# Cosine attention and a leaky-ReLU MLP on one core: row sums inverted on ScalarE, and a new order for batch 2's norms and batch 4's loads

## The chip, the cores and the metric

The kernel runs on one core of a Trainium2 chip. A core has TensorE (PE, matrix products into PSUM), VectorE (DVE), ScalarE (ACT, functions such as exp and ln), GpSimd (POOL) and SyncE (SP, here a queue that issues transfers). They run side by side, each works off its own instructions in order, and semaphores tie them together. Sixteen DMA engines move data. The metric is device time in microseconds of one execution of the whole kernel.

## The reference, cut to what matters

Inputs are q, k and v of shape (8 batches, 12 heads, 448 positions, 64), tau = 0.1, and two weight matrices.

```python
q_n = q / (norm(q, axis=-1) + 1e-06)
k_n = k / (norm(k, axis=-1) + 1e-06)
scores = matmul(q_n, k_n.transpose(0, 1, 3, 2)) / tau
attn = softmax(scores)                    # exp, row sum, division
x = matmul(attn, v)                       # heads put side by side: 3584 x 768
h = x @ w_in                              # 768 -> 2048
out = maximum(0.01 * h, h) @ w_out        # 2048 -> 768
```

The cosine of q and k lies between -1 and 1, so the kernel leaves the maximum out of the softmax: it takes the exponential of ten times the cosine, sums it, and multiplies the product with v by one over the sum.

## The kernel before

**Tiling.** A batch's 448 positions are 4 tiles of 112. Twelve heads make six pairs p and three groups g of two pairs. Per batch the attention runs over twelve *steps* n = 2p + half, and each step handles two of the four key tiles of one pair:

- `scores` (L206, in batch 0 `part_scores`, L224): TensorE multiplies the transposed, normalized k and q (`kT`, `qT`) into PSUM, in two tiles `sc`. The pool of these has two buffers.
- `exponential` (L234): ScalarE turns each tile into `pe`.
- After a group's second pair is through, two entries go into the list `owed`, and the next two steps each take one out with `weigh`. The first (s = 0) makes the group's row sums on TensorE (`sums`, L239 with `ones`), inverts them (`inverse`), makes the first half of the values (`values`, L239 with `v_bf`) and multiplies the two (`x_write`, L283, or L286 and L288 in even batches). The second (s = 1) makes the other half. Sums and values lie in PSUM tiles `pv`, of which there are two: the sums' tile becomes free for the second values when `inverse` has read it, and the first values' tile when `x_write` has. Groups 0 and 1 are weighed at steps 4, 5 and 8, 9 and group 2 at steps 0, 1 of the next batch.

`inverse` has two ways of doing it: in batch 0 ScalarE computes exp(-ln(sum)) (L264, L265), in the seven others VectorE takes the reciprocal (L267).

**The MLP as filling.** `layer1` (L311: six matmuls, then a leaky ReLU on ScalarE, L316) and `layer2` (L324: sixteen matmuls, a copy on ScalarE, L330, and stores from SP, L336) form one long list `dense`. After each step `fill(budget(b, n))` emits as much of it as a fixed budget says. In batches 1 to 7, where nothing is owed and layer 1 is next, a step holds its second exponential until a piece of the filling is out. Layer 1, layer 2 and batch 0 and 1's transposes on TensorE share a PSUM pool `mm` of two tiles. All this order is written at build time: nothing is scheduled while the kernel runs.

**The norms of the next batch.** While one batch is attended to, q and k of the next are made ready, in hand-placed calls after the steps: `early` for batches 0 and 1, `after_scores` for the later ones. The chain for q and for k is:

- `load`: a DMA issued by GpSimd (L92) that also rounds to bf16. `qk_bf` has four buffers, so batch 4's tiles take those of batch 2, once batch 2's multiplies have read them.
- `norm_sums`: squares (L124) and a reduce (L127) on VectorE.
- `norm_root`: ln and exp on ScalarE (L139, L140).
- `norm_inverse` (L144, L145) on VectorE, and `norm_apply` (L152), six multiplies with the inverse norm, on the engine that is handed over: V is VectorE, P is GpSimd.
- `turn`: a transposing DMA issued by SP (L169) into `qT` or `kT`. Scores of batches 2 to 7 wait for both. `turned` first clears a few columns with a memset on GpSimd (L163). Batches 0 and 1 are transposed on TensorE instead (`turn_pair`, L180).

In batch 1, batch 2's q is summed after step 3 and its k after step 5; q's root and its multiplies, on GpSimd, follow at step 6, k's root and its multiplies, on VectorE, at step 7, and both turns after step 9. Batch 4's loads stand at steps 0 and 1 of batch 2, and are the next DMAs on GpSimd's queue after the multiplies of batch 2.

Of the kernel before, what the change touches and what calls it, by code (L numbers as in the profile page):

```python
# [10 lines left out]
ACTF = mybir.ActivationFunctionType  # L11
# [5 lines left out]
def kernel(  # L17
# [18 lines left out]
    nc = tc.nc  # L36
    B, H, S, D = q.shape
# [46 lines left out]
    def load(b, what, g0=0, g1=G):  # L84
        src = {"q": q_r, "k": k_r, "v": v_r}[what]
        if (what, b) not in st:
            if what == "v":
                st[what, b] = vpool.tile([PK, H, NT, D], BF16, name="v_bf")
            else:
                st[what, b] = bfpool.tile([PK, H, NT, D], BF16, name="qk_bf")  # L90
        if g1 - g0 == G:
            nc.gpsimd.dma_start(out=st[what, b], in_=src[b])  # L92
            return
        for g in range(g0, g1):
            nc.gpsimd.dma_start(out=st[what, b][:, g::G], in_=src[b][:, g::G])
# [19 lines left out]
    def norm_squares(b, what, eng, g0=0, g1=G):  # L115
        if (what + "n", b) not in st:
            st[what + "n", b] = inp.tile([PK, G, 2, NT, 2, D], BF16, name=f"{what}_n")
            st[what + "i", b] = small.tile([PK, G, 4, NT], F32, name=f"{what}_ni")
        for g in range(g0, g1):
            x, sq = by_quad(st[what, b])[:, g], squares(b, what, g, g + 1)[:, 0]  # L120
            if eng is nc.scalar:
                nc.scalar.activation(sq, x, func=ACTF.Square)
            else:
                eng.tensor_mul(sq, x, x)  # L124

    def norm_reduce(b, what, g0=0, g1=G):
        nc.vector.tensor_reduce(  # L127
            st[what + "i", b][:, g0:g1].rearrange("p g a t -> p (g a) t"),
            squares(b, what, g0, g1).rearrange("p g a t d -> p (g a) t d"),
            axis=AX.X, op=ALU.add,  # L130
        )

    def norm_sums(b, what, g0=0, g1=G):
        norm_squares(b, what, nc.vector, g0, g1)
        norm_reduce(b, what, g0, g1)

    def norm_root(b, what, g0=0, g1=G):
        ni = st[what + "i", b][:, g0:g1]
        nc.scalar.activation(ni, ni, func=ACTF.Ln, bias=tiny[:PK])  # L139
        nc.scalar.activation(ni, ni, func=ACTF.Exp, scale=0.5)  # L140

    def norm_inverse(b, what, g0=0, g1=G):
        ni = st[what + "i", b][:, g0:g1]
        nc.vector.tensor_scalar_add(ni, ni, 1e-6)  # L144
        nc.vector.reciprocal(ni, ni)  # L145

    def norm_apply(b, what, eng, g0=0, g1=G):
        x, xn, ni = by_quad(st[what, b]), st[what + "n", b], st[what + "i", b]
        for g in range(g0, g1):
            for j in range(2):  # L150
                ni_j = ni[:, g, 2 * j : 2 * j + 2]
                eng.tensor_tensor(  # L152
                    out=xn[:, g, j].rearrange("p t h d -> p h t d"),
                    in0=x[:, g, 2 * j : 2 * j + 2],
                    in1=ni_j.unsqueeze(3).to_broadcast([PK, 2, NT, D]),
                    op=ALU.mult,
                )


    def turned(b, what):  # L160
        if (what + "T", b) not in st:
            xt = tpool.tile([128, NT * HP * PK + 16], BF16, name=f"{what}T")
            nc.gpsimd.memset(xt[:, NT * HP * PK :], 0.0)  # L163
            st[what + "T", b] = xt
        return st[what + "T", b]

    def turn(b, what):
        xn, xt = st[what + "n", b], turned(b, what)
        nc.sync.dma_start_transpose(  # L169
            out=xt[:, : NT * HP * PK].rearrange("p (c n) -> p c n", n=PK),  # L170
            in_=xn.rearrange("p g j t h d -> p (g j t h d)"),
        )
# [72 lines left out]
    def x_place(b):  # L245


        if b % 2 == 0:
            st["x", b] = xpool.tile([128, KT, 512], BF16, name="xT")
            st["x64", b] = cpool.tile([128, KT, 64], BF16, name="x64")  # L250
        else:
            st["x", b] = xpool.tile([128, KT, 512], BF16, name="xT")
            nc.gpsimd.tensor_copy(out=st["x", b][:, :, 0:64], in_=st["x64", b - 1])

    def sums(b, g, c0=0, c1=S):
        sm = ppv.tile([128, S], F32, name="pv")
        columns(sm, b, g, lambda a, ki: ones[:PK, :], c0, c1)
        return sm

    def inverse(b, g, sm, c0=0, c1=S):  # L260
        st["rs", b, g] = wk.tile([128, S], F32, name="rs")
        rs = st["rs", b, g][:, c0:c1]
        if b == 0:
            nc.scalar.activation(rs, sm[:, c0:c1], func=ACTF.Ln)  # L264
            nc.scalar.activation(rs, rs, func=ACTF.Exp, scale=-1.0)  # L265
        else:
            nc.vector.reciprocal(rs, sm[:, c0:c1])  # L267
        if ("x", b) not in st:
            x_place(b)

# [19 lines left out]
    def weigh(b, g, s, c0=0, c1=S):  # L290
        if s == 0:
            inverse(b, g, sums(b, g, c0, c1), c0, c1)
        x_write(b, g, s, values(b, g, s, None, c0, c1), c0, c1)
# [73 lines left out]
    V, P, A = nc.vector, nc.gpsimd, nc.scalar  # L367
# [45 lines left out]
    sm = sums(0, 0, *one)  # L413
# [11 lines left out]
    po = values(0, 0, 0, None, *one)  # L425
    part_scores(2, 1, *one)
    inverse(0, 0, sm, *one)
    part_scores(3, 0, *one)
    part_scores(3, 1, *one)
# [6 lines left out]
    sm = sums(0, 1, *one)  # L436
# [9 lines left out]
    sm = sums(0, 2, *one)  # L446
# [11 lines left out]
    def step(b, what, g0, g1, *steps):  # L458

        for name, eng in steps:  # L460
            if name == "squares":
                norm_squares(b, what, eng, g0, g1)
            elif name == "reduce":
                norm_reduce(b, what, g0, g1)
            elif name == "root":
                norm_root(b, what, g0, g1)
            else:
                norm_inverse(b, what, g0, g1)
                norm_apply(b, what, eng, g0, g1)

    def early(b, n):
        def both(to, g0, g1, name, eq=None, ek=None):
            step(to, "q", g0, g1, (name, eq))
            step(to, "k", g0, g1, (name, ek))

        if b == 0:
            if n == 0:
                both(1, 0, 1, "squares", P, P)
            elif n == 2:
                both(1, 0, 1, "reduce")  # L480
            elif n == 3:
                both(1, 1, 2, "squares", P, P)
            elif n == 4:
                both(1, 0, 1, "root")
            elif n == 5:
                both(1, 0, 1, "apply", V, P)
            elif n == 6:
                both(1, 1, 2, "reduce")
            elif n == 8:
                both(1, 1, 2, "root")  # L490
                both(1, 2, 3, "squares", P, P)
                load(2, "q")
            elif n == 9:
                both(1, 1, 2, "apply", V, P)
                load(2, "k")
            elif n == 11:
                both(1, 2, 3, "reduce")
        elif n == 0:
            both(1, 2, 3, "root")
            load(2, "v")  # L500
        elif n == 1:
            both(1, 2, 3, "apply", V, P)
            load(3, "q")
        elif n == 2:
            load(3, "k")
        elif n == 3:
            norm_sums(2, "q")
        elif n == 5:
            norm_sums(2, "k")
        elif n == 6:  # L510
            step(2, "q", 0, 3, ("root", A), ("apply", P))
        elif n == 7:
            step(2, "k", 0, 3, ("root", A), ("apply", V))
        elif n == 9:
            turn(2, "k")
            turn(2, "q")

    def after_scores(b, n):
        if b < 2:
            return early(b, n)  # L520
        if b + 2 < B and n < 2:
            load(b + 2, "qk"[n])
        if b + 1 == B:
            return
        if n == 2:
            load(b + 1, "v")
            norm_sums(b + 1, "q")
        elif n == 3:
            norm_sums(b + 1, "k")
        elif n == 4:  # L530
            norm_root(b + 1, "q")
        elif n == 5:
            norm_root(b + 1, "k")
            norm_inverse(b + 1, "q")
            norm_apply(b + 1, "q", P)
        elif n == 6:
            norm_inverse(b + 1, "k")
            norm_apply(b + 1, "k", P)
        elif n == 7:
            turn(b + 1, "q")  # L540
        elif n == 9:
            turn(b + 1, "k")
# [21 lines left out]
    for b in range(B):  # L564
        for p in range(HP):
            for half in range(2):
                n = 2 * p + half
# [56 lines left out]
```

## Time and profile before

| | before |
|---|---|
| time, median of 3 (lowest to highest) | 488.46 us (488.28 to 489.73) |
| span of the profiled execution | 487.8 us |
| VectorE, L267, 128x448 | x21, 62.1 us, 2955 ns each |
| ScalarE, L234, 112x896 | x168, 147.0 us, 918 ns each |
| VectorE, L152 (k), all shapes alike, 112x512 | x8, 9.8 us, 1278 ns each |
| GpSimd, L152 (q and k) | x36 and x40, 38.6 and 41.8 us |
| turns into kT and qT, issue to landing | x6 each, median 7.3 and 5.0 us |
| loads of whole q and k tiles, 672 KB, issue to landing | x6 each, median 8.0 and 11.4 us |

How to read the profile. An engine's busy time is that in which it executes, and the idle time before an instruction is put down to what released it last. In a list of waits the three numbers are the total in us, how often, and the longest. A timeline line has its start and its length in us, the engine, the line of the code, the operation, the output and the inputs, and how many instructions are merged into it. The chain of work that ended last is followed back from the end: at each moment it names the work that all later work waited for. PEclk is TensorE's granted clock as a share of the full one. Names of tiles are those of the program.

### The profile page before, as it was taken

To read this page: it belongs to the slowest core of one execution; us is meant where nothing else is said; L and a number is where in the kernel's file an instruction comes from. 1 tells how busy PE (TensorE), PEld (TensorE's weight loads), DVE (VectorE), ACT (ScalarE), POOL (GpSimd) and SP (SyncE) were. 2 spreads that over 40 slices of the span, in tenths; PEclk is the share of its full clock that TensorE was granted. 3 is DMA by queue.
4 is the path that set the end of the run, shared out by engine and by line. 5 is a ranking of instruction groups with operands and counts; after the bars stand their busy time and mean duration, and the time that the engine had idled before them with its cause. 6 is when DMAs were issued, how large, how long until landed. Compare 5 with 4: busy or idle time off the path is not lost.

```text
span 487.8 us, 8428 instructions
## 1 busy us (share of the span) xinstructions
PE 435.2 (89%) x3570; PEld 219.6 (45%) x3584; DVE 214.7 (44%) x255; ACT 273.0 (56%) x457; POOL 127.1 (26%) x146
## 2 busy tenths in 40 slices
PE   0789887564899999997899999999899999999996
PEld 0456553341344544453344544454344544554463
DVE  5935759942852059222952069216813203312000
ACT  3778466532466547843765557754775476543411
POOL 7655560620028010830047010900090000000000
PEclk9999899967899999998999999999999999999999
DMA  9999999097505925296506943343233210020022
GB/s 121 211 202 203 129 163 182 1 130 113 74 0 68 196 67 84 50 127 117 90 1 98 179 77 63 58 104 66 42 56 63 78 50 0 17 65 17 1 65 66
DMA packets 79364, 42.61 MB, mean 87 GB/s; under 512 B 35040, under 2 KB 78560, under 8 KB 79328
## 3 DMA queue, kind: packets, MB, share of 16 engines
q0 software_dynamic: 37728, 22.81, 34.3%
q1 hardware_dynamic: 41600, 19.28, 18.0%
q8 instruction: 28, 0.46, 0.4%
q14 instruction: 8, 0.07, 0.0%
HBM read 45.61 MB, written 11.01 MB: 116 GB/s over the span
## 4 chain that ended last, share of the span: by engine, by line
PE 75%; DMA 11%; DVE 7%; ACT 3%; SPq 2%; issue 1%; POOL 1%; POOLq 0%; ACTq 0%
PE mm L311 28%; PE mm L324 28%; PE pv L239 11%; PE sc L206 7%; DMA w_in_sb<-in_moe_w_in_dram 5%; DMA kT<-k_n 2%; DMA qT<-q_n 2%; DVE k_n L152 2%; ACT pe L234 2%; DMA qk_bf<-in_q_dram 1%; SPq L169 1%; DVE rs L267 1%; DVE q_n L152 1%; ACT hT L316 1%; DVE k_ni L127 1%
## 5 line engine op out<-in xcount | busy, mean ns | idle before, releaser
L234 ACT ACTIVATE pe<-sc 112x896 bf16<-112x896 f32 (+2 forms) x192 | 168.4, 917 | 22.0 <-PE sc L206 13.0
L311 PE MATMUL mm<-xT,w_in_sb 128*128 128x512 bf16 (+3 forms) x850 | 156.2, 334 | 4.2 <-ACT hT L316 1.7
L324 PE MATMUL mm<-w_out_sb,hT 128*128 128x384 bf16 x896 | 154.3, 328 | 0.0
L267 DVE RECIPROCAL rs<-pv 128x448 f32<-128x448 f32 x21 | 62.1, 2955 | 157.4 <-PE pv L239 157.4
L324 PEld LDWEIGHTS <-hT 128*128 128x128 bf16 x896 | 85.0, 98 | 67.8 <-issue 14.7
L311 PEld LDWEIGHTS <-w_in_sb 128*128 128x128 bf16 x864 | 77.6, 99 | 78.4 <-issue 19.8
L316 ACT ACTIVATE hT<-mm 128x512 bf16<-128x512 f32 (+3 forms) x144 | 71.6, 503 | 69.6 <-PE mm L311 69.3
L330 ACT COPY osb<-mm 128x384 f32<-128x384 f32 x56 | 26.8, 479 | 107.6 <-PE mm L324 77.3
L152 POOL TENSOR_TENSOR q_n<-qk_bf,q_ni 112x512 bf16<-112x512 bf16 x36 | 38.6, 1102 | 98.9 <-DVE q_ni L145 82.3
L206 PE MATMUL sc<-qT,kT 64*128 64x448 bf16 (+1 forms) x336 | 50.4, 365 | 14.8 <-ACT pe L234 6.1
L239 PE MATMUL pv<-pe,v_bf 112*32 112x448 bf16 (+2 forms) x864 | 50.0, 355 | 11.1 <-DVE rs L267 10.9
L152 POOL TENSOR_TENSOR k_n<-qk_bf,k_ni 112x512 bf16<-112x512 bf16 x40 | 41.8, 1073 | 6.8 <-DVE k_ni L145 6.8
L92 POOL DMA_DIRECT2D v_bf<-in_v_dram x8 | 7.6, 946 | 115.5 <-PE pv L239 115.3
L239 PEld LDWEIGHTS <-v_bf 112*32 112x32 bf16 x864 | 21.9, 102 | 32.5 <-issue 22.6
L206 PEld LDWEIGHTS <-kT 64*128 64x128 bf16 (+1 forms) x336 | 12.4, 99 | 45.9 <-issue 42.2
L286 DVE TENSOR_TENSOR xT<-pv,rs 128x384 bf16<-128x384 f32 (+2 forms) x30 | 14.1, 477 | 33.7 <-PE pv L239 21.6
L127 DVE TENSOR_REDUCE k_ni<-k_n 112x16 f32<-112x1024 bf16 (+1 forms) x12 | 27.4, 2282 | 0.9 <-POOL k_n L124 0.6
L127 DVE TENSOR_REDUCE q_ni<-q_n 112x16 f32<-112x1024 bf16 (+1 forms) x12 | 27.3, 2279 | 0.3
L239 PE MATMUL pv<-pe,ones 112*32 112x448 bf16 (+2 forms) x432 | 26.3, 364 | 1.1 <-ACT pe L234 1.1
L283 DVE TENSOR_TENSOR xT<-pv,rs 128x448 bf16<-128x448 f32 x24 | 15.0, 625 | 19.5 <-PE pv L239 18.2
L239 PEld LDWEIGHTS <-ones 112*32 112x32 bf16 x432 | 9.6, 101 | 14.8 <-issue 11.2
L180 PE MATMUL mm<-ident,q_n 112*128 112x112 bf16 x48 | 5.6, 254 | 10.8 <-DVE q_n L152 10.5
(50 smaller groups left out, 171.4 us busy)
## 6 DMA issues: line engine op xcount, KB each, us to landing
v_bf<-in_v_dram POOLq DMA_DIRECT2D x8, 672.0 KB, 7.7
qk_bf<-in_q_dram POOLq DMA_DIRECT2D x6, 672.0 KB, 8.0
qk_bf<-in_k_dram POOLq DMA_DIRECT2D x6, 672.0 KB, 11.4
w_in_sb<-in_moe_w_in_dram POOLq DMA_DIRECT2D x4, 768.0 KB, 20.3
w_out_sb<-in_moe_w_out_dram POOLq DMA_DIRECT2D x2, 1536.0 KB, 28.0
out_dram<-osb SPq DMA_DIRECT2D x16, 168.0 KB, 2.2
out_dram<-osb SPq DMA_DIRECT2D x16, 144.0 KB, 2.1
out_dram<-osb SPq DMA_DIRECT2D x16, 120.0 KB, 2.0
```

The costliest lines, as they stand in the source:

```text
L127: nc.vector.tensor_reduce(st[what + "i", b][:, g0:g1].rearrange("p g a t -> p (g a) t"), squares(b, what, g0, g1).rearrange("p g a t d -> ...
L152: eng.tensor_tensor(out=xn[:, g, j].rearrange("p t h d -> p h t d"), in0=x[:, g, 2 * j : 2 * j + 2], in1=ni_j.unsqueeze(3).to_broadcast([P ...
L206: nc.tensor.matmul(out=sc[:wide, a, :S], lhsT=kT[r, o : o + wide], rhs=qT[r, p * S : (p + 1) * S], start=True, stop=True,)
L234: nc.scalar.activation(out=pe, in_=sc, func=ACTF.Exp, scale=inv_tau)
L239: nc.tensor.matmul(out=dst[32 * a : 32 * a + 32, c0:c1], lhsT=weights(a, ki), rhs=st["pe", b, 2 * g + a // 2][:, ki, a % 2, c0:c1], start= ...
L267: nc.vector.reciprocal(rs, sm[:, c0:c1])
L283: nc.vector.tensor_mul(x[:, kt, 64:512], po, rs)
L286: nc.vector.tensor_mul(x[:, kt, c0:c], po[:, c0:c], rs[:, c0:c])
L311: nc.tensor.matmul(out=pm[:, :n], lhsT=w_in_sb[:, kt, m * 128 : (m + 1) * 128], rhs=st["x", b][:, kt, x0 : x0 + n], start=(kt == 0), stop= ...
L316: nc.scalar.activation(out=st["h", c][:, m, :n], in_=pm[:, :n], func=ACTF.Prelu, alpha=0.01)
L324: nc.tensor.matmul(out=po[:, :NH], lhsT=st["h", c][:, m, j0 : j0 + 128], rhs=w_out_sb[:, m, n * NH : (n + 1) * NH], start=(m == 0), stop=( ...
L330: nc.scalar.copy(out=osb, in_=po[:, :NH])
```

## The change

Three edits go together.

1. `inverse` uses ScalarE's ln and exp in every batch. This is to take the long reciprocals off VectorE, and with them the waits of TensorE for the sums' buffer.
2. Batch 2's norms are rearranged inside batch 1. k is summed a step earlier; q's and k's roots come at steps 5 and 6; both sets of multiplies are VectorE's, q's at step 6 and k's at step 7, so that VectorE and GpSimd don't multiply at the same time; q is turned at step 7 as soon as it is through, and k at step 8.
3. Batch 4's loads go from steps 0 and 1 of batch 2 to steps 3 and 4. On GpSimd's queue they then stand behind the load of batch 3's v, and are to run after batch 2's turns rather than beside them.

```diff
     def inverse(b, g, sm, c0=0, c1=S):
         st["rs", b, g] = wk.tile([128, S], F32, name="rs")
         rs = st["rs", b, g][:, c0:c1]
-        if b == 0:
-            nc.scalar.activation(rs, sm[:, c0:c1], func=ACTF.Ln)
-            nc.scalar.activation(rs, rs, func=ACTF.Exp, scale=-1.0)
-        else:
-            nc.vector.reciprocal(rs, sm[:, c0:c1])
+        nc.scalar.activation(rs, sm[:, c0:c1], func=ACTF.Ln)
+        nc.scalar.activation(rs, rs, func=ACTF.Exp, scale=-1.0)
...
         elif n == 3:
             norm_sums(2, "q")
+        elif n == 4:
+            norm_sums(2, "k")
         elif n == 5:
-            norm_sums(2, "k")
+            step(2, "q", 0, 3, ("root", A))
         elif n == 6:
-            step(2, "q", 0, 3, ("root", A), ("apply", P))
+            step(2, "k", 0, 3, ("root", A))
+            step(2, "q", 0, 3, ("apply", V))
         elif n == 7:
-            step(2, "k", 0, 3, ("root", A), ("apply", V))
-        elif n == 9:
+            step(2, "k", 0, 3, ("apply", V))
+            turn(2, "q")
+        elif n == 8:
             turn(2, "k")
-            turn(2, "q")
 
     def after_scores(b, n):
         if b < 2:
             return early(b, n)
-        if b + 2 < B and n < 2:
-            load(b + 2, "qk"[n])
+        n0 = 3 if b == 2 else 0
+        if b + 2 < B and n0 <= n < n0 + 2:
+            load(b + 2, "qk"[n - n0])
```

## The prediction

> **What bounds the kernel now.** I read the page first, for the shares and the clock.
>
> ```profile
> PE 435.2 (89%) x3570; PEld 219.6 (45%) x3584; DVE 214.7 (44%) x255; ACT 273.0 (56%) x457; POOL 127.1 (26%) x146
> ...
> PEclk9999899967899999998999999999999999999999
> ```
>
> TensorE is the bound, and no other engine is near it. The clock row is at 9 nearly everywhere, with one hollow in slices 8 to 10 (98 to 134 us). So I asked for the waits of TensorE, and then for the busy time by stage.
>
> ```profile
> PE pv L239 <- DVE rs L267: 10.9, 3, 8.8
> PE sc L206 <- ACT pe L234: 6.1, 8, 1.2
> PE sc L206 <- DMA qT<-q_n: 5.7, 1, 5.7
> PE sc L206 <- DMA kT<-k_n: 2.5, 1, 2.5
> ```
> ```profile
> 82.00:92.80 10.80, 8.68 (x118) 5.24 (x117) 10.20 (x13) 8.00 (x21) 3.01 (x3) 1.00 0.13 29
> 92.80:101.50 8.70, 0.00 (x0) 0.00 (x0) 8.69 (x6) 1.53 (x2) 7.28 (x8) 0.64 0.14 9
> 101.50:105.20 3.70, 3.66 (x36) 2.34 (x35) 1.25 (x2) 0.56 (x2) 0.00 (x0) 0.50 1.34 181
> 111.00:116.60 5.60, 0.00 (x0) 0.01 (x1) 0.00 (x0) 0.44 (x1) 0.00 (x0) 0.91 1.22 236
> 116.60:127.50 10.90, 10.17 (x72) 3.81 (x72) 7.09 (x7) 3.45 (x4) 0.94 (x1) 0.57 0.15 12
> 240.00:300.00 60.00, 59.73 (x463) 27.82 (x465) 30.16 (x30) 37.11 (x59) 15.46 (x18) 1.00 0.51 86
> ```
>
> Columns: stretch and length, busy us of TensorE, weight loads, VectorE, ScalarE, GpSimd, granted clock, DMA share, GB/s. From 240 us on TensorE is busy 59.7 of 60 us, so there is nothing to win there. The loss lies between 80 and 128 us, at the end of batch 1's attention: two stretches in which TensorE does nothing, each followed by one at a granted clock of 0.50 to 0.57. The VectorE timeline and the chain tell why.
>
> ```profile
> 85.36 3.35 DVE L127 TENSOR_REDUCE k_ni<-k_n 112x48 f32<-112x3072 bf16 x1
> ...
> 90.16 8.47 DVE L152 TENSOR_TENSOR k_n<-qk_bf,k_ni 112x512 bf16<-112x512 bf16 x6
> 98.55 2.94 DVE L267 RECIPROCAL rs<-pv 128x448 f32<-128x448 f32 x1
> ```
> ```profile
> 98.78 7.08 SPq L169
> ...
> 105.97 10.51 DMA qT<-q_n
> ```
>
> Batch 1's second reciprocal stands behind the six k multiplies of batch 2's norms. These take 8.47 us, because GpSimd does the six q multiplies at the same time (89.79 to 98.08). TensorE needs the sums' PSUM buffer, which the reciprocal releases, and stands for 8.8 us. Both turns are issued only at 98.78, together with batch 4's two loads (98.37 and 99.35), so qT lands at 116.48.
>
> **What the Trainium skill says.** "TensorE: Matmul & The Clock Gate", Part 1: after an idle window of about 3.4 us the array runs at half clock until it has been busy for such a window. The trace agrees in kind: 16 value matmuls take 1.68 us after the first stall against 0.93 us at 88.86. It disagrees on the duration: 10.9 us of low clock follow the second stall. "SBUF — State Buffer", SBUF: two separate sides: VectorE with two SBUF inputs and GpSimd lock a shared port pair against each other. The trace agrees: a multiply starts every 1.41 us beside GpSimd (8.47/6) but every 0.645 us alone (1.29 us for two at 66.93), and GpSimd's median is 1.486 us against 1.008 us (6.05/6 at 142.98). "DMA: Bandwidth & Descriptors", Issuing engines are not separate DMA queues: all share 16 DMA engines. The trace agrees: turns land in 15.3 and 10.5 us beside the loads, in 5.0 and 5.6 us without (batches 4 and 3, q). "ScalarE: Activation LUTs", What ACT_TABLE_LOAD costs: 186 ns + 0.833 ns per element, one load for ln and exp together. The trace has 381 and 417 ns at 256 columns for L264 and L265 and a single table load.
>
> **Part 1, the reciprocals.** 21 x 2955 ns = 62.1 us leave VectorE. ScalarE gets 21 pairs. From 192 to 256 columns L264 goes from 330 to 381 ns and L265 from 363 to 417 ns, so at 448 columns I take 381 + 192 x 0.80 = 534 ns and 417 + 192 x 0.84 = 579 ns; the skill's rule gives 559 ns for each. A pair costs some 1.1 us, 23 us in all, and ScalarE goes from 273 to 296 us, 63% of the shorter span. In later batches that is hidden: a step with sums runs about 6.0 us of TensorE work (0.48 scores + 1.63 sums and values + three layer-1 columns of 1.3), while ScalarE then has two exponentials (1.72), three activations (3 x 0.5) and the pair (1.1), 4.3 us. The pair stands behind the exponentials, and ahead of the activations that release layer-1's PSUM, which in the trace begin at about the time at which it would end (156.65 against 156.85 us at batch 2's step 8). I charge 0.5 us for all of batches 2 to 7; the bounds are 0 and 2.
>
> **Part 2, the new order of batch 2's norms.** I follow the queues from 73.7 us, where q's squares start as before (step n is the n-th half-pair of batch 1).
> - Step 4: the sums end at 76.4, and ScalarE, idle from 76.8, inverts them by 77.9. VectorE ends q's sums at 78.9, does x_write, and k's squares and reduce (1.89 + 3.35 - overlap) at 79.5 to 84.7. k's load needs to be there at 79.5: it was issued at 62.56 and landed 9.9 us later.
> - Step 5: the values needn't wait for L267, saving 1.45 us: TensorE is at step 6 by 81.3.
> - Step 6: k's root now waits on ScalarE for the reduce. Behind it are queued step 7's exponentials, and TensorE's next score buffer waits for these. With two exponentials, q's root and two activations ahead of it, ScalarE comes to k's root at 84.7, just as the reduce ends, but the first exponential of step 7 starts at 85.3 rather than at 84.35. The 1.45 us are nearly lost: step 8's second score pair begins at 87.4 against 87.77.
> - Step 8: the pair sits between exponentials and activations and is done at 90.5; layer 1 waits for its PSUM and step 9's scores start at 91.6 against 92.17.
> - VectorE: inverse of q (0.63) and six multiplies alone (6 x 0.645 = 3.9; at 688 ns each, 4.1) to 89.8; the same for k to 94.4. x_write of step 8 follows; its buffer is wanted only in batch 2, so nobody waits.
> - Step 9: the values go at 92.1, not at 101.54. Up to batch 2's first scores the trace has 110.92 - 101.54 = 9.4 us, of which 1.6 are low clock up to 105.2 (0.75 in the values, 0.84 in 18 matmuls: 2.10 against 0.84 for 12). So TensorE is there at 92.1 + 7.8 = 99.9, say 100.3 with the activations' queue.
>
> **Part 3, turns and loads.** qT is issued at 90 and kT at 94.6; nothing else is on the DMA (29 GB/s at 82 to 92.8). Alone a turn landed in 5.0 to 5.6 us: kT is in at 99.6 to 100.2. The two turns overlap by at most a fraction. I take 100.6 for batch 2's first scores against 116.62: **16.0 us**. Without a pause there is no low clock either. The stretch 116.62 to 127.53 then takes 0.48 + 1.63 + 0.48 + 0.87 + 2.71 = 6.2 us, by the later durations in the chain, not 10.9: **4.7 us** (it holds the third L267 wait, 0.71). Batch 4's loads now queue behind batch 3's v at step 3 of batch 2, ahead of the next multiplies on GpSimd by over 15 us. At 8.6 and 14.2 us to landing they are in before batch 3's turn, and norm sums want them a batch later: no cost. Batch 4's own kT wait (2.5 us at 222 to 225) stays, since it collides with batch 6's loads, which don't move.
>
> **Sum.** 16.0 + 4.7 - 0.5 = 20.2; 488.46 - 20.2 = 468.3.
>
> **The rivals.**
> - *The turn takes the stall's place.* kT lands 2 to 4 us later (median of all k turns 7.3), or step 7's wait cascades; TensorE pauses and the low clock returns for 3.7 us or more. For: a 2.5 us wait was enough at 225 us, where the clock is 0.59 for 4 us. Against: the loads are gone. 468.3 + 3 + 3 = 474.
> - *ScalarE becomes the limit in batches 2 to 7.* Most of 18 pairs of 1.1 us comes onto the path: 468.3 + 15 = 483. Against: 37 us of 60 busy.
> - *Slower than before.* All 23 us come onto the path, and the late kT stalls with low clock (6): 468.3 + 23 + 6 = 497. It needs both to fail; nothing in the profile speaks for it but the 6.1 us of waits for L234.
> - *All stalls vanish.* 1.45 + 8.79 + 5.70 + 1.6 + 4.7 = 22.2 and nothing is charged: 466.
>
> **How the numbers follow.** Forecast 0.62, late turn 0.20, everything vanishes 0.11, ScalarE limit 0.04, slower 0.03. The range goes from 465.5 (the last rival with the measurement's width) to 475 (the late turn). Faster 0.96, same 0.01, slower 0.03.
>
> **What would show it.** The wait of L239 for VectorE is gone; the VectorE multiplies of batch 2 take about 0.65 us each and GpSimd's are away; both turns of batch 2 land within 6 us and the first wide scores start at 100 to 101 us with a clock of 1.0; L264 and L265 at 448 columns last 530 to 580 ns; ScalarE's wait for k's reduce is under 1 us. I am wrong if the first wide scores wait for kT by over 2 us, if the low clock is still there after 100 us, or if the waits for L234 and L316 grow by over 2 us after 130 us.

## The result and the profile after

The changed kernel takes 467.75 us (median of 4, 466.62 to 468.35) against 488.37 us before: 20.6 us less, a ratio of 0.958 with a 95% interval of 0.954 to 0.962. The prediction said 468.3 us and a gain of 20.2 us.

Times from here on are those of each kernel's own profile, and line numbers shift in the changed code: L308 and L321 are layers 1 and 2 (before: L311 and L324), L313 and L327 their work on ScalarE, L263 and L264 the ln and exp, L280 and L283 the products with the row sums' inverse. The profile after runs 1.22 us ahead of the one before when step 3 of batch 1 starts (71.78 against 73.00 us), from the loads at the start of the kernel (TensorE's first wait for the weights `w_in` is 0.25 us instead of 1.33). The code up to there is the same in both kernels, so this isn't the work of the change, and stages are compared by their length.

First TensorE's waits in the changed kernel (total us, times, longest):

```profile
PE mm L180 <- DVE q_n L152: 10.8, 2, 10.5
PE sc L206 <- ACT pe L234: 6.5, 9, 1.2
PE sc L206 <- DMA kT<-k_n: 2.3, 1, 2.3
```

The two big waits of before, 10.9 us for the reciprocal and 5.7 us for qT, are not in the list at all. The 10.5 us at the kernel's start and batch 4's wait for kT (2.3 us here, 2.5 us in the kernel before) were there before.

Then four stages, before and after: step 3 to step 9 of batch 1, step 9 to batch 2's first scores, these to batch 2's step 2, and all the rest (columns as in the prediction):

```profile
73.00:92.17 19.17, 14.41 (x176) 8.13 (x174) 18.39 (x20) 12.84 (x25) 2.55 (x3) 1.00 0.73 118
92.17:116.62 24.45, 9.75 (x89) 6.04 (x87) 10.57 (x8) 7.43 (x16) 7.91 (x9) 0.77 0.88 121
116.62:127.53 10.91, 10.20 (x73) 3.80 (x74) 7.12 (x7) 3.45 (x4) 0.94 (x1) 0.58 0.15 12
127.53:487.80 360.27, 348.38 (x2603) 167.27 (x2616) 133.62 (x129) 202.27 (x323) 71.73 (x83) 1.00 0.38 69
```
```profile
71.78:89.94 18.16, 14.62 (x176) 8.16 (x174) 17.92 (x25) 14.76 (x29) 0.25 (x3) 1.00 0.77 125
89.94:98.33 8.39, 8.03 (x88) 4.90 (x86) 3.79 (x7) 6.78 (x15) 0.00 (x0) 1.00 0.95 163
98.33:104.61 6.28, 6.25 (x73) 3.02 (x74) 2.96 (x5) 4.73 (x7) 2.33 (x3) 1.00 0.20 36
104.61:464.90 360.29, 348.67 (x2603) 167.35 (x2616) 81.86 (x111) 220.03 (x359) 72.21 (x84) 0.99 0.41 73
```

The gain is 1.0 us in the first stage, 16.1 in the second and 4.6 in the third, and nothing in the 360 us after it. The rest loses 52 us of VectorE (133.6 to 81.9) and gains 18 us of ScalarE (202.3 to 220.0), and its length doesn't move by 0.1 us. These 21.7 us and the 1.22 us at the start make up the 22.9 us between the two profiled spans. The medians lie only 20.6 us apart: the profiled runs took 489.77 and 466.62 us, the long end of the one kernel's runs and the short end of the other's.

VectorE in the changed kernel, where the reciprocal stood behind 8.47 us of multiplies:

```profile
80.14 3.35 DVE L127 TENSOR_REDUCE k_ni<-k_n 112x48 f32<-112x3072 bf16 x1
...
84.64 3.70 DVE L152 TENSOR_TENSOR q_n<-qk_bf,q_ni 112x512 bf16<-112x512 bf16 x6
...
88.96 3.70 DVE L152 TENSOR_TENSOR k_n<-qk_bf,k_ni 112x512 bf16<-112x512 bf16 x6
92.58 1.15 DVE L280 TENSOR_TENSOR xT<-pv,rs 128x448 bf16<-128x448 f32 x2
```

Twelve multiplies on one engine (8.0 us with the inverse between them) take no longer than six on each of two engines did (8.47 us), and q is through after the first half. The two products at 92.58 come late, and no one waits for them. SP's queue and TensorE's arrival at batch 2 show that both then come out at the same moment:

```profile
88.49 3.26 SPq L169 DMA_TRANSPOSE qT<-q_n  x1
92.73 3.92 SPq L169 DMA_TRANSPOSE kT<-k_n  x1
```
```profile
95.63 2.77 PE L321 MATMUL mm<-w_out_sb,hT 128*128 128x384 bf16 x16
98.33 0.55 PE L206 MATMUL sc<-qT,kT 64*128 64x448 bf16 x4
98.82 0.94 PE L239 MATMUL pv<-pe,ones 112*32 112x448 bf16 x16
```

The turns land 5.1 and 5.3 us after issue, kT thus at 98.0 us; TensorE is there at 98.3.

### The profile page after: what moved, and what is told of

Same layout as the page of the kernel before. It is cut to its first block, busy times and chain, and to the rows that moved or that the text cites. A ratio compares the mean times of both kernels' runs of the same rounds, so it can differ in the third digit from the quotient of the medians.

```text
span 464.9 us, 8442 instructions
## 1 busy us (share of the span) xinstructions
PE 429.8 (92%) x3570; PEld 217.6 (47%) x3584; DVE 151.4 (33%) x240; ACT 293.3 (63%) x499; POOL 118.7 (26%) x140
## 4 chain that ended last, share of the span: by engine, by line
PE 81%; DVE 7%; ACT 5%; DMA 3%; issue 1%; POOL 1%; SPq 0%; POOLq 0%; ACTq 0%; DVEq 0%
PE mm L308 30%; PE mm L321 30%; PE pv L239 12%; PE sc L206 8%; ACT pe L234 4%; DMA kT<-k_n 2%; DVE q_n L152 2%; DVE k_ni L127 1%; PE sc L224 1%; DVE q_ni L127 1%; PE mm L180 1%; ACT hT L313 1%; DMA qk_bf<-in_q_dram 1%; DVE q_ni L144 1%; DVE q_n L124 1%
## 5 line engine op out<-in xcount | busy, mean ns | idle before, releaser
L234 ACT ACTIVATE pe<-sc 112x896 bf16<-112x896 f32 (+2 forms) x192 | 168.4, 918 | 11.2 <-PE sc L224 7.6
L308 PE MATMUL mm<-xT,w_in_sb 128*128 128x512 bf16 (+3 forms) x850 | 155.6, 332 | 3.0 <-ACT hT L313 1.5
L321 PE MATMUL mm<-w_out_sb,hT 128*128 128x384 bf16 x896 | 154.4, 328 | 0.0
L321 PEld LDWEIGHTS <-hT 128*128 128x128 bf16 x896 | 85.0, 98 | 67.9 <-issue 14.7
L308 PEld LDWEIGHTS <-w_in_sb 128*128 128x128 bf16 x864 | 76.8, 98 | 77.0 <-issue 18.9
L313 ACT ACTIVATE hT<-mm 128x512 bf16<-128x512 f32 (+3 forms) x144 | 71.4, 502 | 48.1 <-PE mm L308 47.3
L327 ACT COPY osb<-mm 128x384 f32<-128x384 f32 x56 | 26.8, 479 | 96.6 <-PE mm L321 92.3
L206 PE MATMUL sc<-qT,kT 64*128 64x448 bf16 (+1 forms) x336 | 49.4, 357 | 9.3 <-ACT pe L234 6.5
L283 DVE TENSOR_TENSOR xT<-pv,rs 128x384 bf16<-128x384 f32 (+2 forms) x30 | 14.1, 477 | 126.8 <-ACT rs L264 93.7
L280 DVE TENSOR_TENSOR xT<-pv,rs 128x448 bf16<-128x448 f32 x24 | 14.8, 623 | 124.2 <-PE mm L308 47.3
L152 POOL TENSOR_TENSOR q_n<-qk_bf,q_ni 112x512 bf16<-112x512 bf16 x30 | 30.3, 1040 | 79.6 <-DVE q_ni L145 79.6
L239 PE MATMUL pv<-pe,v_bf 112*32 112x448 bf16 (+2 forms) x864 | 47.8, 344 | 0.2 <-ACT rs L263 0.2
L239 PE MATMUL pv<-pe,ones 112*32 112x448 bf16 (+2 forms) x432 | 24.5, 343 | 0.8 <-ACT pe L234 0.8
L180 PE MATMUL mm<-ident,q_n 112*128 112x112 bf16 x48 | 5.6, 254 | 11.0 <-DVE q_n L152 10.8
L264 ACT ACTIVATE rs<-rs 128x448 f32<-128x448 f32 (+2 forms) x27 | 14.4, 535 | 0.9
```

The source lines that it names most:

```text
L152: eng.tensor_tensor(out=xn[:, g, j].rearrange("p t h d -> p h t d"), in0=x[:, g, 2 * j : 2 * j + 2], in1=ni_j.unsqueeze(3).to_broadcast([P ...
L206: nc.tensor.matmul(out=sc[:wide, a, :S], lhsT=kT[r, o : o + wide], rhs=qT[r, p * S : (p + 1) * S], start=True, stop=True,)
L234: nc.scalar.activation(out=pe, in_=sc, func=ACTF.Exp, scale=inv_tau)
L239: nc.tensor.matmul(out=dst[32 * a : 32 * a + 32, c0:c1], lhsT=weights(a, ki), rhs=st["pe", b, 2 * g + a // 2][:, ki, a % 2, c0:c1], start= ...
L280: nc.vector.tensor_mul(x[:, kt, 64:512], po, rs)
L283: nc.vector.tensor_mul(x[:, kt, c0:c], po[:, c0:c], rs[:, c0:c])
```

## The experiments

The theory: two stalls follow one another, the sums' buffer behind VectorE's queue and the turns beside the loads, and each leaves TensorE at a low clock. Removing the first lets the second grow. The main rivals: the reciprocals alone were the cost; or the loads alone; or ScalarE's added work takes part of the gain back.

### The three edits apart

**Edit 1 alone**, on the kernel before:

```diff
-        if b == 0:
-            nc.scalar.activation(rs, sm[:, c0:c1], func=ACTF.Ln)
-            nc.scalar.activation(rs, rs, func=ACTF.Exp, scale=-1.0)
-        else:
-            nc.vector.reciprocal(rs, sm[:, c0:c1])
+        nc.scalar.activation(rs, sm[:, c0:c1], func=ACTF.Ln)
+        nc.scalar.activation(rs, rs, func=ACTF.Exp, scale=-1.0)
```

> The kernel before with edit 1 alone: row sums on ScalarE, batch 2's norms and batch 4's loads as before. Theory (two stalls in a row, the second set by the turns): the 8.8 us wait for the sums' buffer goes, but both turns still start when VectorE is through with k's multiplies, at about 97 us, and run beside batch 4's loads, so they land at 113 to 115 us and TensorE waits some 14 us there instead of 8.8 + 5.7, with the low clock after it. 486 to 488 us, a gain of 0 to 2 us. Rival (the reciprocals were the cost, 62 us of VectorE with TensorE waiting behind them): 468 to 475 us.

Measured: 484.12 us, ratio 0.993 (0.990 to 0.996). The first stall is gone and the second has eaten it; TensorE's waits in this kernel:

```profile
PE sc L206 <- DMA qT<-q_n: 13.9, 1, 13.9
PE mm L180 <- DVE q_n L152: 10.6, 1, 10.6
```

13.9 us instead of 8.8 + 5.7, as expected. kT landed 14.2 us and qT 9.4 us after issue. The time is 2 us below what was expected, and the profile has it in the stretch after the wait: 7.8 us from batch 2's first scores to its step 2 (113.25 to 121.07), not 10.9. The rival that all 62 us of reciprocals counted is out.

**Edit 3 alone**, on the kernel before:

```diff
-        if b + 2 < B and n < 2:
-            load(b + 2, "qk"[n])
+        n0 = 3 if b == 2 else 0
+        if b + 2 < B and n0 <= n < n0 + 2:
+            load(b + 2, "qk"[n - n0])
```

> The kernel before with edit 3 alone. Theory: the 8.8 us wait for the sums' buffer stays, but the turns issued at 98.8 us land alone, by 108 us, before TensorE is there at 110.9; the 5.7 us wait and the low clock after it go: 478 to 480 us. Rival (the turns are late because they are issued late): 486 to 488 us.

Measured: 481.99 us, ratio 0.989 (0.986 to 0.993), 2 us short of the expectation. The turns land in 5.3 and 6.8 us and TensorE doesn't wait for them. The rival is out. But the stretch after batch 2's first scores takes 9.75 us:

```profile
110.32 0.55 PE L206 MATMUL sc<-qT,kT 64*128 64x448 bf16 x4
...
114.80 0.94 PE L239 MATMUL pv<-pe,v_bf 112*32 112x448 bf16 x16 [1.82 <-DVE rs L267]
115.68 4.46 PE L324 MATMUL mm<-w_out_sb,hT 128*128 128x384 bf16 x16
```

With TensorE at full clock here (1.00 from 110.32 to 115.68), the third reciprocal is less hidden: the wait for it is 1.82 us, not 0.71. A low clock follows this wait (0.61 from 115.68 to 120.07): the 16 layer-2 matmuls take 4.46 us instead of the 2.77 of full clock.

**Edits 2 and 3**, the changed kernel with the VectorE reciprocal back (the reverse of the first diff):

> The changed kernel with edit 1 taken back: VectorE's reciprocal in batches 1 to 7, edits 2 and 3 kept. Theory: batch 1's second reciprocal stands behind both sets of multiplies and ends at about 100 us, TensorE waits 6 to 7 us for the sums' buffer, then runs 9.4 us to batch 2's first scores at about 109 us, where the turns are long there. 477 us, about half of the gain. Rival A (the new order alone does it): 468. Rival B (the reciprocal alone does it): 488.

Measured: 480.44 us, ratio 0.984 (0.978 to 0.990), 3 us over the expectation. TensorE's waits in this kernel:

```profile
PE pv L239 <- DVE rs L267: 6.9, 3, 3.6
PE sc L206 <- ACT pe L234: 6.0, 8, 1.2
PE mm L311 <- ACT hT L316: 3.4, 2, 3.0
```

The second reciprocal ended at 100.0 and batch 2's first scores went at 109.19, both as worked out. The wait divides otherwise: 3.0 us of it is earlier, because ScalarE stands at k's root until VectorE is through with k's reduce, which the first reciprocal has delayed by 3 us. What was missed comes afterwards, the same 1.82 us and slow layer-2 block as with edit 3 alone (9.75 us again, against 6.28 in the changed kernel). So edit 2 leans on edit 1: with reciprocals on VectorE, the earlier root blocks ScalarE.

**Edits 1 and 2**, the changed kernel with batch 4's loads back at steps 0 and 1:

```diff
-        n0 = 3 if b == 2 else 0
+        n0 = 0
```

> The changed kernel with edit 3 taken back: batch 4's loads at steps 0 and 1 of batch 2. Theory: GpSimd issues them as soon as batch 2's multiplies have read the tiles, at about 88 and 93 us, beside the turns, which land in 10 to 15 us instead of 5.1 and 5.3. Batch 2's first scores go at 104 to 107 us instead of 98.3, followed by the low clock (4 us more): 476 to 480 us. Rival (the turns were late only because they were issued late, the loads beside them cost little): 468 to 470 us.

Measured: 477.29 us, ratio 0.978 (0.972 to 0.984), as expected. GpSimd issues the loads at 88.90 and 93.21 us, each some 0.2 us after a turn; qT lands in 9.4 and kT in 14.0 us. TensorE's waits, and the stretches around the wait for kT:

```profile
PE sc L206 <- DMA kT<-k_n: 9.8, 2, 7.3
```
```profile
99.80:107.06 7.26, 0.00 (x1) 0.01 (x2) 0.00 (x0) 0.48 (x1) 0.00 (x0) 0.85 1.21 194
107.06:111.00 3.94, 3.94 (x36) 1.24 (x36) 0.00 (x0) 2.84 (x4) 0.00 (x0) 0.50 0.00 0
```

**Edits 1 and 3**, the old order of batch 2's norms:

> The changed kernel with edit 2 taken back: edits 1 and 3 with the old order of batch 2's norms. Theory: k's multiplies still run beside GpSimd's, the turns are issued at 96.5 and 100 us and the second lands at 105 us, where TensorE has been waiting since 99.4 us, with some low clock after it: 475 to 477 us. Rival (the new order adds nothing once the loads are away): 467 to 470 us.

Its edits are the first two diffs together. Measured: 474.06 us, ratio 0.973 (0.970 to 0.977), 1 us below the expectation. The turns land in 5.3 and 5.1 us, but are issued only at 96.51 and 99.95 us, and TensorE waits for the second:

```profile
PE sc L206 <- DMA qT<-q_n: 5.8, 1, 5.8
```

In us saved of 488, by the ratios: edit 1 alone 3.6, edit 3 alone 5.2, 1 and 3 13.0, 1 and 2 10.8, 2 and 3 7.8, all three 20.5. What an edit is worth depends on which of the others is there: edit 1 brings 3.6 us alone and 12.7 us as the last of the three.

### GpSimd's share of the multiplies

```diff
             step(2, "k", 0, 3, ("root", A))
-            step(2, "q", 0, 3, ("apply", V))
+            step(2, "q", 0, 3, ("apply", P))
```

> The changed kernel with q's multiplies of batch 2 on GpSimd again, at the new place, so that they run beside VectorE's for k. Theory[...]: six k multiplies take 8.5 us and six q multiplies 8.7 us, both from about 84.7 us, so both turns are issued at 93.5 to 97 us and kT lands at about 102 us, 3.6 us after TensorE is there; with some low clock 471 to 475 us. Rival (no contention; GpSimd is only slower, 1.0 us each): q is through at 91 us, k at 89 us, kT lands by 99.5 us, 468 to 469 us.

Measured: 472.54 us, ratio 0.969 (0.963 to 0.976), as the theory had it. GpSimd's and VectorE's multiplies in this kernel:

```profile
84.77 7.85 POOL L152 TENSOR_TENSOR q_n<-qk_bf,q_ni 112x512 bf16<-112x512 bf16 x6 [13.27 <-PE sc L206]
```
```profile
86.38 7.39 DVE L152 TENSOR_TENSOR k_n<-qk_bf,k_ni 112x512 bf16<-112x512 bf16 x6
```

1.23 us each on VectorE and 1.31 on GpSimd, against 0.62 and 1.01 alone. kT lands at 101.3 us, 3.3 us later than in the changed kernel, and TensorE waits 2.2 us:

```profile
101.37 0.55 PE L206 MATMUL sc<-qT,kT 64*128 64x448 bf16 x4 [2.16 <-DMA kT<-k_n]
101.85 0.94 PE L239 MATMUL pv<-pe,ones 112*32 112x448 bf16 x16
```

Dividing the work over two engines that hinder each other costs some 5 us by the medians. The profiled run, with 470.2 us the shortest of the five, shows some 3 us of it, in the start of batch 2's first scores (101.37 against 98.33 us). The low clock that was expected after the wait isn't in this profile (1.00 from 101.37 to 112 us), so where the other 2 us of the median go is open.

### Is the low clock an echo of the idle time?

The kernel before, with matmuls that do nothing for the result in the two idle stretches:

```diff
+    def busy(n):
+        pm = pmm.tile([128, 512], F32, name="mm")
+        for _ in range(n):
+            nc.tensor.matmul(
+                out=pm, lhsT=w_in_sb[:, 0, 0:128],
+                rhs=w_in_sb[:, 1, 0:512], start=True, stop=True,
+            )
...
+                if (b, n) == (2, 0):
+                    busy(30)
                 hold = b > 0 and not owed and dense[at[0]][1] < 2.0
...
+                if (b, n) == (1, 9):
+                    busy(38)
                 if owed:
                     weigh(*owed.pop(0))
```

> The kernel before with 68 matmuls more, whose results nothing reads: 38 of 512 columns ahead of step 9's values in batch 1 and 30 ahead of batch 2's first scores, where TensorE stands still. Theory (the low clock is the echo of the idle stretches): TensorE stays at the full clock, step 9's stretch gets 1.6 us shorter, which the wait for the turns takes up again, and the stretch after batch 2's first scores takes 7 us instead of 10.9: 483 to 485 us, faster with more work. Rival (the clock has other causes, or the matmuls are in the way): 488 to 490 us.

Measured: 485.12 us, ratio 0.995 (0.993 to 0.997): faster with 68 matmuls more, and 0.1 us above the range that was expected. Stretches of this kernel over the two stalls and the time after the second:

```profile
92.50:101.50 9.00, 9.00 (x48) 3.93 (x44) 9.00 (x6) 2.26 (x4) 8.11 (x9) 1.00 0.07 4
101.50:111.00 9.50, 8.78 (x89) 5.51 (x89) 1.78 (x3) 5.37 (x12) 0.00 (x0) 1.00 1.37 157
111.00:117.00 6.00, 5.38 (x25) 2.23 (x23) 0.00 (x0) 0.00 (x0) 0.00 (x0) 1.00 1.29 232
117.00:128.00 11.00, 8.49 (x84) 3.73 (x85) 8.76 (x7) 5.37 (x8) 0.93 (x1) 1.00 0.36 47
```

The granted clock is 1.00 in all four, so the low clock of these stretches does come from standing still. The stretch from batch 2's first scores to its step 2 takes 8.07 us (117.31 to 125.38) instead of 10.91; with nothing waited for it is 6.28 us in the changed kernel. The difference is one wait of 1.82 us for the third reciprocal, which the slow matmuls had partly covered before:

```profile
121.80 0.94 PE L239 MATMUL pv<-pe,v_bf 112*32 112x448 bf16 x16 [1.82 <-DVE rs L267]
122.68 2.77 PE L324 MATMUL mm<-w_out_sb,hT 128*128 128x384 bf16 x16
```

So of the 4.63 us won in this stretch, 2.84 us are the clock and 1.8 us the reciprocal, if the clock is mended first. The division depends on that: with edit 3 alone the same wait of 1.82 us was followed by the low clock, and the stretch took 9.75 us, 3.5 us more than in the changed kernel, so that the reciprocal was worth 3.5 us there. Why the low clock follows the wait there and not here, the runs don't show.

### What the row sums cost on ScalarE in batches 2 to 7

VectorE's reciprocal for batches 2 to 7 only:

```diff
-        nc.scalar.activation(rs, sm[:, c0:c1], func=ACTF.Ln)
-        nc.scalar.activation(rs, rs, func=ACTF.Exp, scale=-1.0)
+        if b < 2:
+            nc.scalar.activation(rs, sm[:, c0:c1], func=ACTF.Ln)
+            nc.scalar.activation(rs, rs, func=ACTF.Exp, scale=-1.0)
+        else:
+            nc.vector.reciprocal(rs, sm[:, c0:c1])
```

> The changed kernel with ScalarE's inverse in batches 0 and 1 alone, and VectorE's reciprocal in batches 2 to 7, as before. Theory (only batch 1's three row sums matter, since in later batches neither engine is waited for): 467 to 469 us, like the changed kernel. Rival (the later 18 reciprocals were part of the gain): 470 to 478 us. Rival (ScalarE's pairs cost something there): 464 to 466 us.

Measured: 466.28 us, ratio 0.957 (0.953 to 0.961), not to be told from the changed kernel's 0.958. Eighteen of the 21 moved reciprocals bring and cost nothing that these runs can tell. How close ScalarE is to costing something, two more kernels tell, which repeat each ln and exp in batches 2 to 7 once and three times (range(4) in the second):

```diff
-        nc.scalar.activation(rs, sm[:, c0:c1], func=ACTF.Ln)
-        nc.scalar.activation(rs, rs, func=ACTF.Exp, scale=-1.0)
+        for _ in range(2 if b > 1 else 1):
+            nc.scalar.activation(rs, sm[:, c0:c1], func=ACTF.Ln)
+            nc.scalar.activation(rs, rs, func=ACTF.Exp, scale=-1.0)
```

> The changed kernel with the ln and exp of each row sum done twice in batches 2 to 7 (18 pairs more, written over by the same result). Theory (the pair is hidden behind TensorE's filling there): 18 x 1.1 us = 20 us more of ScalarE and 0 to 2 us more of time, 468 to 470 us. Rival (ScalarE's work is on the path, and the forecast held because something else was gained): 475 to 488 us.

> The changed kernel with the ln and exp of each row sum done four times in batches 2 to 7 (54 pairs more, 59 us of ScalarE). Theory: a step with sums now has 4.4 us of pairs ahead of layer 1's activations, and TensorE, with two PSUM tiles of lead, waits about 1.9 us in each such step in which layer 1 is the filling, some 12 of 18: 480 to 492 us. If it stays below 472 us, the slack is larger than the step sum says.

Measured: 474.54 us, ratio 0.971 (0.967 to 0.976), and 522.18 us, ratio 1.070 (1.064 to 1.076). Both expectations fell: one pair more costs 6.8 us, three cost 54.4 us, a whole microsecond for each pair. ScalarE and TensorE at step 4 of batch 2, and TensorE at step 4 of batch 3 (172.00), with one pair more (line numbers are one higher here):

```profile
112.38 0.56 ACT L264 ACTIVATE rs<-pv 128x448 f32<-128x448 f32 x1
...
113.58 0.55 ACT L264 ACTIVATE rs<-pv 128x448 f32<-128x448 f32 x1
114.15 0.58 ACT L265 ACTIVATE rs<-rs 128x448 f32<-128x448 f32 x1
...
115.14 1.07 ACT L314 ACTIVATE hT<-mm 128x512 bf16<-128x512 f32 x2
```
```profile
112.38 2.76 PE L309 MATMUL mm<-xT,w_in_sb 128*128 128x512 bf16 x12
115.77 1.46 PE L309 MATMUL mm<-xT,w_in_sb 128*128 128x512 bf16 x6 [0.63 <-ACT hT L314]
...
172.00 1.14 PE L309 MATMUL mm<-xT,w_in_sb 128*128 128x384 bf16 x6 [1.13 <-ACT hT L314]
```

TensorE fills two PSUM tiles and stands before the third until ScalarE has read the first. The second pair starts 1.20 us after the first (112.38 and 113.58), and TensorE stands 0.63 us, so a single pair leaves some 0.6 us of slack at this step. It isn't the same at each: with one pair more TensorE waits like this at steps 4 and 8 of all six batches, 0.20 to 1.13 us each time, and 7.3 us in all. By the same reckoning (an estimate) a single pair leaves 1.0 us where the wait is shortest, and less than 0.1 us at step 4 of batches 3 and 5, where it is 1.13 us. The step's sum (4.3 of 6.0 us) had said 1.7 us.

Three more pairs make a wait of 2.99 us at step 4 of batch 2, and the six matmuls after it take 2.72 us; after the same wait in batch 4 they take 1.46:

```profile
119.77 2.72 PE L309 MATMUL mm<-xT,w_in_sb 128*128 128x512 bf16 x6 [2.99 <-ACT hT L314]
...
244.09 1.46 PE L309 MATMUL mm<-xT,w_in_sb 128*128 128x512 bf16 x6 [2.99 <-ACT hT L314]
```

So the low clock comes on top of some of these waits, though not of all (mean granted clock of the run 0.963 against 0.99).

### The same edit for batch 6's loads

```diff
-        n0 = 3 if b == 2 else 0
+        n0 = 3 if b % 2 == 0 else 0
```

> The changed kernel with batch 6's loads moved in the same way, to steps 3 and 4 of batch 4, away from batch 4's k turn. Theory: that turn lands in about 5 us instead of 11.2, TensorE's 2.3 us wait for it goes, and the low clock after it, 1.05 us in 16 layer-2 matmuls and 0.6 us in 16 value matmuls: 463.5 to 465 us. Rival (the loads then hold up something later, or the turn is late for another reason): 467 to 469 us.

Measured: 463.17 us, ratio 0.9495 (0.946 to 0.953), 25 us faster than before and better than the changed kernel (the intervals don't overlap). Batch 4's k turn lands in 5.0 us, and TensorE around it is busy without a gap at full clock:

```profile
189.00:196.00 7.00, 7.00 (x57) 3.40 (x55) 0.62 (x1) 4.21 (x6) 0.00 (x0) 1.00 0.54 110
196.00:206.00 10.00, 10.00 (x97) 4.65 (x96) 0.62 (x1) 6.60 (x11) 0.00 (x0) 1.00 0.28 75
```

The last kernel joins this with VectorE's reciprocal in batches 2 to 7 (the diff above):

> The version with batch 6's loads moved as well, and ScalarE's inverse in batches 0 and 1 alone. Theory (in later batches the choice of the engine is free): 462 to 464 us, the same as with ScalarE everywhere, 463.2. Rival (ScalarE's pairs cost something in later batches, as 466.3 against 467.8 us may hint): 460.5 to 462 us.

Measured: 463.62 us, ratio 0.951 (0.948 to 0.954): no difference from the one before it, which again says that the engine of the later row sums is free to choose.

## Why the prediction was right

The mechanism held in its main steps, the stall behind VectorE's queue, the turns beside the loads and the low clock after both. The argument for ScalarE's slack did not, and one stretch was divided wrongly. That the sum of 20.2 us comes within 0.4 us of the medians is in part luck: the stages of the two profiles give 21.7 us, 1.5 us more, since two terms were small misses in the same direction (1.05 and 0.5 us), and the four runs of the kernel before lie up to 3.7 us apart. Point by point, in stages from step 3 of batch 1:

- **The new order.** Batch 2's first scores were put 27.6 us after step 3's scores (100.6 - 73.0); they came after 26.55 us. The 1.05 us are in small terms: the multiplies start every 0.62 us rather than 0.645, step 9 came 0.4 us earlier, and kT landed sooner for it. k's root waited 0.27 us for the reduce (under 1 us was said), and the first exponential of step 7 started at 84.10 us, which is 85.32 on the clock of before, against the 85.3 us of the working. The 1.45 us won at step 5 were partly lost there, as worked out: 1.0 us of them were left at step 9, where the working had 0.6.
- **Turns and loads.** 5.1 and 5.3 us against 5.0 to 5.6. That the loads were the cause of the 15.3 and 10.5 us is shown from both sides: moved away from turns issued late (edit 3 alone), these land in 5.3 and 6.8 us; put back beside turns issued early, 9.4 and 14.0 us, and 9.5 us of time.
- **The stretch after it.** 6.28 us against 6.2 worked out, 4.63 us won against 4.7. The size was right, but its two parts were mis-sized: the kept-busy kernel has the reciprocal's share at 1.8 us rather than the 0.71 us that the wait showed, and the clock's at 2.8 us. The wait before had been measured against a slow TensorE. Nor was the clock low for all of the 10.9 us: it is 0.50 from 116.62 to 125.5 us, and 0.98 from 125.8 on.
- **ScalarE's 23 us.** Charged at 0.5 us for batches 2 to 7; it is 0 within what the measurement tells. L263 and L264 take 559 and 577 ns at 448 columns, where 186 ns + 0.833 ns per element, from the Trainium skill's "ScalarE: Activation LUTs", What ACT_TABLE_LOAD costs, makes an estimate of 559 ns, and the extrapolation gave 534 and 579; a pair holds ScalarE for 1.07 us (100.42 to 101.49). But the first argument for it was wrong: slack is not a step's TensorE work less its ScalarE work. It is how long ScalarE may keep the first of two PSUM tiles, and of that between less than 0.1 and 1.0 us is left. The second argument, that the pair ends about when the activations that release layer 1's PSUM begin, named the right place, at one step. The one pair still fits at all of them, at the tightest by luck.
- **The rivals.** "The turn takes the stall's place" is what edits 1 and 2 do without edit 3 (477.3 us) and what GpSimd's share of the multiplies does (472.5). "ScalarE becomes the limit" is what one more pair begins (474.5) and three more are (522.2).

What stays open: in the kernel before, the low clock after the second stall lasts some 9 us in the profiled run, with edit 1 alone some 4 us after a longer stall (there the 0.71 us wait for the reciprocal in the middle of it is missing too). The runs show that it follows standing still, and neither which waits it follows nor what sets how long it lasts. Edit 2 alone wasn't tried, nor what the 1.2 us waits for L234 at step 3 would bring if they were removed.

## What to carry to other kernels

When two stalls follow one another on the bounding engine, work out where each would land if the other were gone: here edits 1 and 3 alone brought 0.7% and 1.1% and the three together 4.2%. Judge whether an added operation is hidden by the next buffer that is waited for, and how much of its lead is left, and not by an engine's share of busy time (ScalarE was at 63% of the span, and at some steps less than 0.1 us from being waited for). Ask of each bulk load what it runs beside: moving two loads by three steps took two transfers from 10 to 15 us back to 5 to 7, and doing the same in one more place gave another 4 us.

## What the runs showed of the hardware

- In the kernel before, TensorE's granted clock was 0.50 after waits of 8.8 and 5.7 us, and the kernel gets faster, by 0.5%, if 68 useless matmuls keep TensorE from standing still (clock 1.00).
- The length of a wait alone doesn't tell whether the low clock follows. It followed a wait of 1.82 us with edit 3 alone (clock 0.61) and one of 2.99 us with three more pairs (six matmuls of 128x512 in 2.72 us). It didn't follow one of 1.82 us in the kept-busy kernel, one of 2.16 us with q on GpSimd, and another of 2.99 us with three more pairs (1.46 us).
- On a TensorE at low clock part of a wait is covered by slower matmuls: the same reciprocal is waited for 0.71 us before and 1.82 us at full clock.
- Twelve multiplies of 112x512 on VectorE alone took 8.0 us with an inverse between them, and six each on VectorE and GpSimd at the same time 8.5 and 8.3 us.
